# Attention and a mixture of experts on one core: the last three slot tiles behind a branch on the count of tiles in use

## The chip, the core and the metric

The kernel runs on one core of one Trainium2 chip. The metric is the time of one execution in device microseconds (us). Three timed runs of the kernel before gave 283.19, 280.19 and 283.39 us, median 283.19. The profile is of one more execution of 279.71 us.

## What is computed

A chunked attention (32 heads in 4 batches of 8, 768 positions, 64 channels) feeds a mixture of experts over 3072 tokens of 512 channels. Each token goes through a dense two-layer network and through one of 8 experts, chosen by the largest gate logit. The reference, cut to what matters here:

```python
x = attn_out.transpose(0, 2, 1, 3).reshape(B * S, H * D)     # 3072 tokens x 512
y_dense = np.maximum(x @ w1_dense, 0.0) @ w2_dense
logits = x @ w_gate
expert_idx = np.argmax(logits, axis=1)
gate_w = softmax(logits)[np.arange(N), expert_idx]
for e in range(8):
    mask = expert_idx == e
    h = np.maximum(x[mask] @ w1[e], 0.0)
    y_moe[mask] = gate_w[mask, None] * (h @ w2[e])
return y_dense + y_moe
```

The inputs are the same draw each time (a fixed seed), so each expert gets the same tokens in every execution.

## The kernel before

**Order of the work.** All five engines are scheduled by hand: within an engine instructions run in the order in which the kernel's Python emits them. The engines are PE (matrix products), DVE and ACT (element-wise), POOL (element-wise, and DMAs whose descriptors it makes itself), and SP (which here only issues DMAs).

**First 180 us.** The attention of 16 pairs of heads, the dense layers, and the gate. For each token a record (its activations in bf16, its gate weight, its number, its dense result) is written to a table `x_rec` in DRAM, in the row of its expert's region (`row_out`, L480 to L495).

**Slot tiles.** The experts then work on tiles of 128 rows of that table. How the tokens fall on the experts is known only on the chip, so the program holds the largest number of tiles that can be needed: `NS` = 24 + 8 - 1 = 31 slots. The slots come in two rounds. The first round has `R1` = 11 slots (0 to 10), for tiles that the first three batches fill completely; the second has `R2` = 20 (11 to 30), for all that is left. A slot that gets no rows is computed too: it reads some rows, and its destinations lie outside the output, so its scatter writes nothing.

For each slot two lists on the chip give the first row of its tile in `x_rec` and its expert. They come from the counts per expert: `lists_1a` and `lists_1b` for round one, `lists_2a` (L579), `lists_2b` (L586) and `lists_2c` (L608) for round two. `experts_of` (L507) returns `cum`, the running sum of tiles over the experts; its last entry is the count of tiles of that round. The row lists, expert lists and destination offsets are small tiles in SBUF.

An engine that needs an entry as an address reads it into registers: `entry` (L627) loads up to 8 values in one instruction (TENSOR_LOAD; in the profile its line is L632) and hands them out slot by slot. In round one that is 8 and 3 values, in round two 8, 8 and 4; PE, DVE and SP each do it.

One slot s is worked on in these steps:

- `fetch(s)` (L650, SP): a DMA of 128 rows, 385 KB, from `x_rec` into one of the rooms (`room`, L643; round two has 12).
- `transposed(s)` (L672): PE transposes the activations in four pieces into PSUM (`at_ps`, L679), ACT copies them to `xT` (L683).
- `staged(s)` (L686, DVE): copies the expert's first weights to `w_st` (L690); three buffers.
- `first_layer(s)` (L693): 16 matmuls into PSUM (`sc`, L698), then ReLU on ACT (`h_sb`, L703).
- `second_layer(s)` (L706): 4 matmuls with the expert's second weights, at a register's address (`av`, L711), on POOL the destinations (`dst`, L719), on DVE the weighted sum `y` with the dense result (L724), on POOL the scatter of the rows to the output (L727).

In the loop of a round the steps are interleaved: first layer of s, transposes and staging of s + 2, second layer of s - 1, a fetch for a later slot. The first twelve fetches of round two, and staging and transposes of its first two slots, stand ahead of its loop (L907 to L911):

```python
for s in range(R1, NS):
    first_layer(s)
    if s + 2 < NS:
        transposed(s + 2)
        staged(s + 2)
    if s > R1:
        second_layer(s - 1)
        if s - 1 + 2 * T < NS:
            fetch(s - 1 + 2 * T)
second_layer(NS - 1)
```

After the last slot each engine drains and meets the others at a barrier (rows of L948); SP waits there for every DMA's semaphore.

Of the kernel before, what the change touches and what calls it, by code (L numbers as in the profile page):

```python
# [14 lines left out]
ALU = mybir.AluOpType  # L15
AX = mybir.AxisListType
I32 = mybir.dt.int32
# [3 lines left out]
def kernel(  # L21
# [14 lines left out]
    nc = tc.nc  # L36
# [12 lines left out]
    T = S // 128  # L49
# [3 lines left out]
    PE_, DVE_ = mybir.EngineType.PE, mybir.EngineType.DVE  # L53
    ACT_, POOL_, SP_ = (
        mybir.EngineType.Activation, mybir.EngineType.Pool, mybir.EngineType.SP
    )
# [3 lines left out]
    E = moe_w_gate.shape[1]  # L60
# [30 lines left out]
    NS = NT + E - 1  # L91

    R1 = -(-((N_tokens - S) - E * 127) // 128)
    R2 = NS - R1
    r_pool = ctx.enter_context(tc.tile_pool(name="r_pool", bufs=1))

    def iota_f32(n, name, base=0, step=1, cm=0):
# [26 lines left out]
    with (  # L124
# [372 lines left out]
        lst = {}  # L497
# [9 lines left out]
        def experts_of(cnt, n, add):  # L507

            cnt_i = r_work.tile([128, E], I32, tag="cnt_i")
            nc.vector.tensor_scalar(cnt_i, cnt, add, None, ALU.add)  # L510
            nc.vector.tensor_scalar(cnt_i, cnt_i, 7, None, ALU.logical_shift_right)
            tl = r_work.tile([128, 1, E], F32, tag="tl")
            nc.vector.tensor_copy(tl[:, 0], cnt_i)
            part = r_work.tile([128, E, E], F32, tag="part")
            nc.vector.tensor_tensor(part, upto, tl.to_broadcast([128, E, E]), ALU.mult)
            cum = r_work.tile([128, E, 1], F32, tag="cum")
            nc.vector.reduce_sum(cum, part, axis=AX.X)

            en = r_work.tile([128, R2, E], F32, tag="en")
            en = en[:, :n]  # L520
            nc.vector.tensor_tensor(
                en, slot_no[:, :n, None].to_broadcast([128, n, E]),
                cum.rearrange("p e o -> p o e").to_broadcast([128, n, E]), ALU.is_ge,
            )
            ef = r_work.tile([128, R2], F32, tag="ef")
            ef = ef[:, :n]
            nc.vector.reduce_sum(ef, en, axis=AX.X)
            return tl[:, 0], cum, en, ef

        def of_expert(val, en, n, tag):  # L530

            step = r_work.tile([128, 1, E], F32, tag="step")
            nc.vector.tensor_tensor(step[:, 0], val[:, 1:], val[:, :E], ALU.subtract)
            big = r_work.tile([128, R2, E], F32, tag="big")
            big = big[:, :n]
            nc.vector.tensor_tensor(big, en, step.to_broadcast([128, n, E]), ALU.mult)
            got = r_work.tile([128, R2], F32, tag=tag)
            got = got[:, :n]
            nc.vector.reduce_sum(got, big, axis=AX.X)
            return got  # L540
# [38 lines left out]
        def lists_2a():  # L579
# [3 lines left out]
            nc.vector.tensor_tensor(cnt, cnt_ps, low[:, :E], ALU.subtract)  # L583
            lst["b"] = cnt_ps, experts_of(cnt, R2, 127.0)

        def lists_2b():  # L586
            cnt_ps, (tl, cum, en, ef) = lst.pop("b")

            org = r_work.tile([128, E + 1], F32, tag="org")
            nc.vector.memset(org[:, E:], 0.0)  # L590
            nc.vector.scalar_tensor_tensor(
                org[:, :E], cum[:, :, 0], -128.0, cnt_ps, op0=ALU.mult, op1=ALU.add
            )
            rb = of_expert(org, en, R2, "rb")
            nc.vector.scalar_tensor_tensor(
                rb, rb, org[:, 0:1], slot_row[:, :R2], op0=ALU.add, op1=ALU.add
            )

            nc.vector.scalar_tensor_tensor(
                rb, ef, float(E), rb, op0=ALU.is_lt, op1=ALU.mult  # L600
            )
            rb_i = r_pool.tile([128, R2], I32, name="rb_2")
            nc.vector.tensor_copy(rb_i, rb)
            et_i = r_pool.tile([128, R2], I32, name="et_2")
            nc.vector.tensor_scalar(et_i, ef, float(E - 1), None, ALU.min)
            lst["c"] = rb, en, rb_i, et_i

        def lists_2c():  # L608
# [34 lines left out]
        def room(s):  # L643

            if s < R1:
                return bat[B - 2]["rec"], s % T
            j = (s - R1) % (2 * T)
            return bat[B - 1 if j < T else B - 2]["rec"], j % T

        def fetch(s):  # L650
            row = entry(SP_, 0, s, r_sp, N_rows - 128)
            xg, t = room(s)
            ins = nc.sync.dma_start(xg[:, t, :], x_rec[bass.ds(row, 128), :])
            if s in (0, R1):
                while rows_written:
                    tc.add_manual_dep(
                        ins.ins, rows_written.pop(),
                        mybir.DependencyInfo(
                            mybir.DependencyClass.Sync, mybir.DependencyReason.DATA
                        ),  # L660
                        reason="the rows in DRAM",
                    )
            elif s < R1:
                for f in rows_written:
                    tc.declare_no_dep(
                        ins.ins, f, reason="tiles of this round are full without these"
                    )
            xgs[s] = xg, t
            if s < R1:
                first_round.append(ins.ins.name)  # L670

        def transposed(s):  # L672
            xtp = at_b[:, 2 * (s % 2):2 * (s % 2) + 2, :].rearrange(
                "p a (d t) -> p (a d) t", t=128
            )
            xg, t = xgs[s]
            xgb = xg.bitcast(BF16)
            for d in range(DT):
                nc.tensor.transpose(  # L679
                    xtp[:, d, :], xgb[:, t, d * 128:(d + 1) * 128], identity  # L680
                )
            xT = m_work.tile([128, DT, 128], BF16, tag="xT")
            nc.scalar.copy(xT, xtp)  # L683
            xTs[s] = xT

        def staged(s):  # L686

            e = entry(DVE_, 1, s, e_dve, E - 1)
            w_st = w_work.tile([128, DT, F], BF16, tag="w_st")
            nc.vector.tensor_copy(w_st[:, None], w1_all[:, bass.ds(e, 1), :, :])  # L690
            w_sts[s] = w_st

        def first_layer(s):  # L693
            xT, w = xTs.pop(s), w_sts.pop(s)
            ph = sc[:, s % 2, :].rearrange("p (f t) -> p f t", t=128)
            for f in range(FT):
                for d in range(DT):
                    nc.tensor.matmul(  # L698
                        ph[:, f, :], w[:, d, f * 128:(f + 1) * 128], xT[:, d, :],
                        start=(d == 0), stop=(d == DT - 1),  # L700
                    )
            h_sb = m_work.tile([128, FT, 128], BF16, tag="h")
            nc.scalar.activation(h_sb, ph, AF.Relu)  # L703
            hs[s] = h_sb

        def second_layer(s):  # L706
            h_e = hs.pop(s)
            py = av[:, s % 2, :]
            e = entry(PE_, 1, s, e_pe, E - 1)
            for f in range(FT):  # L710
                nc.tensor.matmul(  # L711
                    py, h_e[:, f, :], w2_all[:, bass.ds(e, 1), f, :],
                    start=(f == 0), stop=(f == FT - 1),
                )
            xg, t = xgs.pop(s)
            s0, _, _, _, far_i = lists[s >= R1]

            dst = y_work.tile([128, 1], I32, tag="dst")
            nc.gpsimd.tensor_tensor(  # L719
                dst, xg.bitcast(I32)[:, t, GW + 1:GW + 2], far_i[:, s - s0:s - s0 + 1],  # L720
                ALU.add,
            )
            y = y_work.tile([128, D_moe], F32, tag="y")
            nc.vector.scalar_tensor_tensor(  # L724
                y, py, xg[:, t, GW:GW + 1], xg[:, t, YD:], op0=ALU.mult, op1=ALU.add
            )
            ins = nc.gpsimd.indirect_dma_start(  # L727
                out, bass.IndirectOffsetOnAxis(ap=dst, axis=0), y, None,
                bounds_check=N_tokens - 1, oob_is_err=False,
            )  # L730
            scattered(ins, "out")
# [177 lines left out]
        for s in range(R1, R1 + 2):  # L909
            staged(s)  # L910
            transposed(s)  # L911
        for s in range(R1, NS):
            first_layer(s)
            if s + 2 < NS:
                transposed(s + 2)
                staged(s + 2)
            if s > R1:
                second_layer(s - 1)
                if s - 1 + 2 * T < NS:
                    fetch(s - 1 + 2 * T)  # L920
        second_layer(NS - 1)
        moe.close()


# [28 lines left out]
```

## Time and profile before

| | us |
|---|---|
| median of three timed runs | 283.19 |
| lowest, highest of them | 280.19, 283.39 |
| the profiled execution | 279.71 |
| its span, first to last instruction | 278.0 |
| PE busy | 208.4 (75%) |
| DVE busy | 158.7 (57%) |
| ACT busy | 134.8 (48%) |
| POOL busy | 136.0 (49%) |
| mean granted clock of PE | 0.93 of full speed |

How to read the profile's lines. A group or piece names the engine, the source line, the operation and the tiles it writes and reads; an engine's name with a q is its sequencer, which waits, loads registers and issues, while the engine itself idles. In brackets stands the idle time of the engine before an instruction and what ended it. The chain is the work that ended last, followed back from the last instruction; each piece of it starts when the one before it releases it, and "issue" is time for which the profile shows no releaser.

### The profile page before, as it was taken

How to read it: one execution, taken by the hardware profiler on the slowest of the kernel's cores; microseconds unless marked ns; L12 is line 12 of the kernel's file. 1: busy time of each engine (PE TensorE's matmuls, PEld its weight loads, DVE VectorE, ACT ScalarE, POOL GpSimd, SP SyncE). 2: the span in 40 equal slices, each digit the busy share in tenths (PEclk: the TensorE clock that was granted, in tenths of full speed). 3: DMA queues.
4: the chain of work that ended last, by engine and by line, in shares of the span. 5: the costliest groups of instructions: out<-in, count | busy, mean ns of one | idle time of the engine just before them, and what ended most of it. 6: DMA issues, size and time to landing. Idle time of an engine off the chain costs nothing.

```text
span 278.0 us, 10776 instructions
## 1 busy us (share of the span) xinstructions
PE 208.4 (75%) x4528; PEld 156.1 (56%) x4559; DVE 158.7 (57%) x321; ACT 134.8 (48%) x204; POOL 136.0 (49%) x210
## 2 busy tenths in 40 slices
PE   1487569539878859598686986869879968999970
PEld 1365547337656547375455765637656646777740
DVE  3575476445674566546537575674585555676740
ACT  2273565516556546265535556426653525555520
POOL 8055155512376673075445144640846654756561
PEclk9999795968999988889978699999999999999996
DMA  6999989995999999988999299896988999893310
GB/s 103 187 119 188 194 141 168 199 195 105 183 198 163 223 161 226 194 202 150 191 180 215 39 212 398 205 218 204 346 202 243 309 397 403 265 335 148 120 59 0
DMA packets 59440, 55.51 MB, mean 200 GB/s; under 512 B 35966, under 2 KB 51326, under 8 KB 59392
## 3 DMA queue, kind: packets, MB, share of 16 engines
q0 software_dynamic: 20560, 31.49, 54.7%
q1 hardware_dynamic: 38832, 23.33, 34.9%
q8 instruction: 36, 0.59, 0.9%
q14 instruction: 12, 0.10, 0.1%
HBM read 51.62 MB, written 20.74 MB: 260 GB/s over the span
## 4 chain that ended last, share of the span: by engine, by line
PE 51%; issue 16%; DMA 12%; DVE 9%; ACT 5%; SPq 3%; POOL 1%; POOLq 0%; DVEq 0%; ACTq 0%
DMA vw<-in_v_dram 7%; PE sc L698 7%; PE ph L460 7%; PE av L711 6%; PE pd L474 6%; PE av L311 5%; PE at_ps L299 4%; PE tp_f L241 4%; PE xtt L355 4%; DMA out_dram<-y,dst 3%; PE at_ps L370 2%; PE at_ps L679 2%; PE sc L275 2%; SPq L217 2%; ACT h_d L467 2%
## 5 line engine op out<-in xcount | busy, mean ns | idle before, releaser
L485 POOL DMA_INDIRECT x_rec<-rec_b,row_i x24 | 24.9, 1036 | 50.7 <-issue 28.7
L727 POOL DMA_INDIRECT out_dram<-y,dst x31 | 31.3, 1009 | 27.7 <-DVE w_st L690 12.9
L724 DVE SCALAR_TENSOR_TENSOR y<-av,rec_b 128x512 f32<-128x512 f32 x31 | 23.3, 750 | 23.8 <-PE av L711 17.7
L284 DVE TENSOR_REDUCE mx<-sc 128x12 f32<-128x768 f32 x16 | 15.3, 957 | 35.3 <-PE sc L275 35.3
L698 PEld LDWEIGHTS <-w_st 128*128 128x128 bf16 x496 | 30.2, 98 | 8.3 <-DVE w_st L690 1.1
L698 PE MATMUL sc<-xT,w_st 128*128 128x128 bf16 x496 | 32.8, 219 | 1.6 <-DVE w_st L690 0.9
L311 PE MATMUL av<-vw,at 64*32 64x65 f32 x1536 | 22.6, 240 | 15.1 <-issue 15.0
L711 PE MATMUL av<-w_all,h_sb 128*128 x112 | 30.5, 379 | 4.5 <-DVE y L724 2.4
L703 ACT ACTIVATE h_sb<-sc 128x512 bf16<-128x512 f32 x31 | 18.5, 597 | 31.4 <-PE sc L698 31.4
L311 PEld LDWEIGHTS av<-vw,at 64*32 64x32 f32 x1536 | 18.1, 112 | 23.5 <-issue 22.5
L474 PE MATMUL pd<-w2d,h_d 128*128 128x512 bf16 x77 | 24.7, 396 | 5.3 <-DVE rec_b L478 3.9
L198 ACT COPY vw<-vw 24x1536 f32<-24x1536 f32 x16 | 23.5, 1468 | 9.2 <-DMA vw<-in_v_dram 8.9
L460 PE MATMUL ph<-xTb_b,w1d 128*128 128x128 bf16 x384 | 27.2, 227 | 1.0 <-issue 1.0
L460 PEld LDWEIGHTS <-w1d 128*128 128x128 bf16 x384 | 24.8, 102 | 4.3 <-issue 1.4
L345 POOL CAST rec_b<-x_p 128x768 bf16<-128x768 f32 x16 | 13.4, 838 | 25.6 <-DVE x_p L323 19.2
L363 POOL CAST xTb_b<-xT 128x768 bf16<-128x768 f32 x15 | 12.5, 832 | 22.9 <-ACT xT L358 22.9
L355 PE MATMUL xtt<-identity_f,x_p 128*128 128x128 f32 x96 | 18.0, 314 | 6.8 <-ACT h_d L467 3.1
L253 DVE COPY dT<-tp_f 128x768 bf16<-128x768 bf16 x16 | 15.3, 954 | 13.6 <-PE tp_f L241 13.3
L690 DVE COPY w_st<-w_all 128x2048 bf16 x31 | 21.2, 694 | 2.6 <-issue 2.5
L478 ACT COPY rec_b<-pd 128x512 f32<-128x512 f32 x16 | 9.4, 585 | 25.9 <-PE pd L474 21.1
L251 ACT COPY dT<-tp_f 128x768 bf16<-128x768 bf16 x16 | 12.7, 795 | 18.2 <-PE tp_f L241 18.0
L291 ACT ACTIVATE a_sb<-dif 128x768 f32<-128x768 f32 x16 | 13.5, 845 | 16.1 <-DVE dif L286 16.1
(231 smaller groups left out, 381.6 us busy)
## 6 DMA issues: line engine op xcount, KB each, us to landing
rec_b<-x_rec SPq DMA_DIRECT2D x31, 385.0 KB
w_all<-in_moe_w_dram POOLq DMA_DIRECT2D x16, 512.0 KB, 10.8
vw<-in_v_dram SPq DMA_DIRECT2D x32, 184.0 KB
x_rec<-rec_b SPq DMA_DIRECT2D x1, 3080.0 KB
vw<-in_mem_v_dram SPq DMA_DIRECT2D x32, 48.0 KB
vw<-in_v_dram SPq DMA_DIRECT2D x64, 4.0 KB
w1d<-in_moe_w_dense_dram POOLq DMA_DIRECT2D x1, 512.0 KB
w2d<-in_moe_w_dense_dram POOLq DMA_DIRECT2D x1, 512.0 KB
```

The costliest lines, as they stand in the source:

```text
L198: copy(vt[p0 + CHUNK:p0 + CTX, :NCH, :D], vt[p0:p0 + CTX - CHUNK, 1:NCH + 1, :D],)
L311: nc.tensor.matmul(av[cc * CHUNK:(cc + 1) * CHUNK, hh, t * (D + 1):(t + 1) * (D + 1)], at[p0:p0 + KEYS, t, cc * CHUNK:(cc + 1) * CHUNK], v ...
L355: nc.tensor.transpose(xtt[:, t * 128:(t + 1) * 128], xb[:, t0 + t, :], identity_f32)
L460: nc.tensor.matmul(ph[:, f * 128:(f + 1) * 128], w1d_sb[:, d, f * 128:(f + 1) * 128], xTb[:, d, t * 128:(t + 1) * 128], start=(d == 0), st ...
L474: nc.tensor.matmul(pd, h_d[:, f * 128:(f + 1) * 128], w2d_sb[:, f, :], start=(f == 0), stop=(f == FT - 1),)
L485: ins = nc.gpsimd.indirect_dma_start(x_rec, bass.IndirectOffsetOnAxis(ap=row_i[:, n:n + 1], axis=0), bat[b]["rec"][:, t, :], None,)
L690: nc.vector.tensor_copy(w_st[:, None], w1_all[:, bass.ds(e, 1), :, :])
L698: nc.tensor.matmul(ph[:, f, :], w[:, d, f * 128:(f + 1) * 128], xT[:, d, :], start=(d == 0), stop=(d == DT - 1),)
L703: nc.scalar.activation(h_sb, ph, AF.Relu)
L711: nc.tensor.matmul(py, h_e[:, f, :], w2_all[:, bass.ds(e, 1), f, :], start=(f == 0), stop=(f == FT - 1),)
L724: nc.vector.scalar_tensor_tensor(y, py, xg[:, t, GW:GW + 1], xg[:, t, YD:], op0=ALU.mult, op1=ALU.add)
L727: ins = nc.gpsimd.indirect_dma_start(out, bass.IndirectOffsetOnAxis(ap=dst, axis=0), y, None, bounds_check=N_tokens - 1, oob_is_err=False,)
```

## The change

A constant `NS_MOST` = NS - 3 = 28 is added. In `lists_2b`, DVE computes `used`, the count of tiles in use in both rounds (the last entry of `cum` plus R1), as an integer. Ahead of the second round's loop each of the five engines loads that one value into a register. The loop becomes a function of its first and last slot; it runs once for slots 11 to 27, with fetches up to slot 27. Slots 28, 29 and 30 stand behind a branch that every engine takes for itself, on `used` > 28: three fetches, staging and transposes of the first two, then the same function. In the arm that skips them each engine adds to its semaphores what the body would have added, so that the waits behind it hold in both cases.

In the order of each engine this puts the new load: on PE between the first weight load and the first matmul of slot 11's first layer; on DVE ahead of the staging of slot 13; on ACT ahead of the ReLU of slot 11; on POOL ahead of the destinations of slot 11; on SP behind the fetch of slot 22. The branch stands behind each engine's last instruction for slot 27. The body holds 157 instructions of PE, 15 of DVE, 12 of ACT, 16 of POOL and 13 of SP.

```diff
     R2 = NS - R1
+    NS_MOST = NS - 3
...
             nc.vector.tensor_scalar(et_i, ef, float(E - 1), None, ALU.min)
+
+            used = r_pool.tile([128, 1], I32, name="used")
+            nc.vector.tensor_scalar(used, cum[:, E - 1], float(R1), None, ALU.add)
+            lst["used"] = used
             lst["c"] = rb, en, rb_i, et_i
...
         for s in range(R1, R1 + 2):
             staged(s)
             transposed(s)
-        for s in range(R1, NS):
-            first_layer(s)
-            if s + 2 < NS:
-                transposed(s + 2)
-                staged(s + 2)
-            if s > R1:
-                second_layer(s - 1)
-                if s - 1 + 2 * T < NS:
-                    fetch(s - 1 + 2 * T)
-        second_layer(NS - 1)
+        def slot_tiles(first, end):
+            for s in range(first, end):
+                first_layer(s)
+                if s + 2 < end:
+                    transposed(s + 2)
+                    staged(s + 2)
+                if s > first:
+                    second_layer(s - 1)
+                    if first < NS_MOST and s - 1 + 2 * T < NS_MOST:
+                        fetch(s - 1 + 2 * T)
+            second_layer(end - 1)
+
+        any_more = nc.values_load(
+            lst.pop("used")[0:1, 0:1], engines=(PE_, DVE_, ACT_, POOL_, SP_),
+            min_val=0, max_val=NS,
+            skip_runtime_bounds_check_because="a count of tiles",
+        )
+        slot_tiles(R1, NS_MOST)
+
+        with tc.If(any_more > NS_MOST):
+            for s in range(NS_MOST, NS):
+                fetch(s)
+            for s in range(NS_MOST, NS_MOST + 2):
+                staged(s)
+                transposed(s)
+            slot_tiles(NS_MOST, NS)
         moe.close()
```

## The prediction

> **What bounds the kernel now.** I read the page first (span, chain), then the stretches from 203 us on, the chain in order of time, and the rows of the last instructions. By the page the chain that ends last is half TensorE:
>
> ```profile
> span 278.0 us, 10776 instructions
> PE 51%; issue 16%; DMA 12%; DVE 9%; ACT 5%; SPq 3%; POOL 1%; POOLq 0%; DVEq 0%; ACTq 0%
> ```
>
> The edit touches only what runs after about 203 us, so two stretches matter. The columns are length, then busy time per engine, clock, DMA share, GB/s.
>
> ```profile
> 232.00:264.00 32.00, 31.55 (x379) 24.25 (x386) 21.68 (x32) 17.11 (x33) 19.45 (x30) 1.00 0.69 241
> 264.00:272.00 8.00, 5.33 (x46) 3.13 (x45) 3.03 (x5) 1.90 (x4) 4.97 (x9) 1.00 0.16 55
> ```
>
> From 232 to 264 PE is busy 31.55 of 32.00 us at a granted clock of 1.00: the second round of slot tiles is bound by PE alone, and no other engine is near full. One slot tile is three pieces in the chain:
>
> ```profile
> 258.68 0.89 PE sc L698 x16
> 259.58 0.22 PE at_ps L679 x4
> 259.80 0.86 PE av L711 x4
> 260.66 0.89 PE sc L698 x16
> ```
>
> From one first layer to the next is 260.66 - 258.68 = 1.98 us. What a slot tile less is worth is read here: 1.98 us each.
>
> **Is the branch skipped?** The body runs if more than 28 tiles are in use. In the drawn inputs, by the reference's routing, the experts take 339, 581, 96, 448, 352, 375, 288 and 593 tokens; of the first 2304 tokens 128, 495, 96, 352, 288, 160, 288, 497. Round one takes full tiles in order until it has 11 (1, 3, 0, 2, 2, 1, 2, 0). What is left, rounded up to tiles, is 2, 2, 1, 2, 1, 2, 1, 5 = 16, so 27 are used. The first expert has exactly 128 early tokens; one fewer gives 27 too. The trace agrees. Of the last five output scatters the first two and the last, and what the DMA engines moved from 265 to 278 us in 40 slices of 0.325 us:
>
> ```profile
> 264.21 0.99 POOL L727 DMA_INDIRECT out_dram<-y,dst  x1 [0.78 <-DVE w_st L690]
> 266.19 0.98 POOL L727 DMA_INDIRECT out_dram<-y,dst  x1 [0.77 <-POOL dst L719]
> ...
> 271.79 0.99 POOL L727 DMA_INDIRECT out_dram<-y,dst  x1 [0.66 <-POOL dst L719]
> GB/s 25 0 290 378 139 0 0 0 2 0 0 0 0 0 2 0 0 0 0 0 2 0 0 0 0 1 1 0 0 0 0 0 0 0 0 0 0 0 0 0
> ```
>
> The burst at 265.65 to 266.6 belongs to the scatter of 264.21 (slot 26); the four scatters after it (slots 27 to 30) move nothing. So 27 tiles hold rows, 27 > 28 is false, and slots 28, 29 and 30 go.
>
> **The change, part by part.**
>
> *Three slot tiles removed.* They carry 48 + 12 matmuls in the first and second layer, 12 transposes, six ACT operations, six DVE ones, three scatters on POOL, and three fetches of 385 KB on SP. All but PE's lie beside PE (stretch above), so they cost and give nothing by themselves. The last two slots of the list have no successor to transpose or stage; slots 26 and 27 now take that form, so the tail keeps its shape and moves up by 3 x 1.98 = 5.94 us. Term: -5.94.
>
> *One DVE operation, `used`, 128x1, in the list stage.* It stands behind L605 and ahead of the staging copy:
>
> ```profile
> 203.65 0.17 DVE L605 TENSOR_SCALAR et<-ef 128x20 int32<-128x20 f32 x1
> 203.72 0.69 DVE L690 COPY w_st<-w_all 128x2048 bf16 x1
> 204.62 0.75 DVE L724 SCALAR_TENSOR_TENSOR y<-av,rec_b 128x512 f32<-128x512 f32 x1 [0.21 <-PE av L711]
> ```
>
> At most 0.17 us, and DVE idles 0.21 us before the y that waits for PE, which covers it. Without that cover 0.17 us would enter the chain. Term: 0.
>
> *A register load on each engine.* Where these land decides their price. In the program's order PE's load stands between the weight load of the first matmul of slot 11 (which waits for DVE's staged weights) and that matmul. That is the head of the second round, where the chain reads:
>
> ```profile
> 227.86 0.70 DVE w_st L690
> 228.56 0.05 issue
> 228.61 1.08 PE sc L698 x16
> ...
> 230.42 1.05 PE sc L698 x16
> 231.47 0.22 PE at_ps L679 x4
> 231.70 0.44 issue
> 232.13 0.81 PE av L711 x3
> 232.94 0.89 PE sc L698 x16
> ```
>
> PE waits here for w_st until 228.56, and only then can its sequencer reach the new load. Sixteen matmuls stand behind it, ACT waits for those, and from 232 on PE never idles again, so nothing absorbs the delay: the load is paid in full. The 0.44 us of issue at 231.70 is such a load of eight values, partly covered. The rows of the loads that exist (ns min/median/max; then single ones on PE, of eight values at 230.9 and 246.9 and of four at 262.8):
>
> ```profile
> L632 SPq TENSOR_LOAD <-rb x5: 302/685/1031, 182.5 to 240.7; - x5
> L632 DVEq TENSOR_LOAD <-et x5: 346/601/1740, 193.1 to 256.8; - x5
> L632 PEldq TENSOR_LOAD <-et x5: 332/812/1139, 202.3 to 262.8; - x5
> L632 PEldq TENSOR_LOAD <-et x1: 812/812/812, 230.9 to 230.9; - x1
> L632 PEldq TENSOR_LOAD <-et x1: 587/587/587, 246.9 to 246.9; - x1
> L632 PEldq TENSOR_LOAD <-et x1: 332/332/332, 262.8 to 262.8; - x1
> ```
>
> Eight values less four are 255 ns, 64 ns a value; one value in the quiet end would be 332 - 3 x 64 = 140 ns. That is the lower bound. The upper is the longest load of the trace, 1.74 us. At 230.9, nearest in time and on the same engine, eight values took 0.22 us over the quiet 587 ns; I add 0.25 us for that, and 0.05 us of issue: 0.45 us. Ends kept: 0.14 and 1.74. Term: +0.45.
>
> The Trainium skill, page "Runtime: NRT & Kernel Launch", section "Instruction fetch mechanics", puts a register load at about 200 ns per register even in bulk. The trace disagrees for further values (64 ns); by that figure the term would be an estimated 0.2 us and the gain 0.25 us larger.
>
> The other four loads are hidden, each by its own idle time:
>
> ```profile
> 229.77 0.60 ACT L703 ACTIVATE h_sb<-sc 128x512 bf16<-128x512 f32 x1 [1.40 <-PE sc L698]
> L653 SPq EVENT_SEMAPHORE  x9: 511/1377/4717, 225.9 to 246.2; - x9
> 234.57 0.98 POOL L727 DMA_INDIRECT out_dram<-y,dst  x1 [4.01 <-DMA rec_b<-x_rec]
> ```
>
> ACT idles 1.40 us where its load comes (only one over 1.40 would show). SP's load stands behind the twelfth fetch of the round, where SP next waits 4.72 us for a free room; the five fetches queued behind it lose nothing. POOL's stands ahead of slot 11's scatter, which waits 4.01 us anyway. DVE's stands ahead of the third staging copy; that one is first needed for slot 13 at 232.94, three microseconds later. Term: 0; uncovered, each costs at most the 1.74 above.
>
> *The branch.* Each engine compares and jumps over its body; in the skip arm it adds what the body would have added to its semaphores, and POOL posts one INC_SWDGE_SEM. The trace has no taken branch. The places are all at an engine's end, so the covers are the drains:
>
> ```profile
> L948 POOLq DRAIN  x3: 51/111/5620, 271.6 to 277.7; - x3
> L948 PEldq DRAIN  x2: 13/332/652, 269.6 to 277.5; - x2
> L937 POOLq INC_SWDGE_SEM  x1: 31/31/31, 0.2 to 0.2; - x1
> ```
>
> POOL's drain sets the end: it begins at 271.57, before the last scatter, and ends at 277.19, 4.4 us after that scatter's operation (271.79 + 0.99). PE is there over six microseconds earlier (269.6), ACT and DVE like it; SP jumps even earlier. Only POOL's branch can count. Lower bound 0, if the drain is counted from the scatter; upper bound a fetch of code that nothing covers. For that the nearest rows are a page of code and a DMA's landing in the quiet end:
>
> ```profile
> q8 instruction: 36, 0.59, 0.9%
> DMA to landing us min/median/max: 2.1/2.4/2.7
> ```
>
> 0.9% of 16 x 278 us over 36 packets is 1.1 us a page; 2.7 us is the upper bound. I take 0.1 us, since over 1 us of sequencer time lies beside the scatter. A negative cost I exclude: the skip arm only adds.
>
> **Sum**: -5.94 + 0.45 + 0 + 0.1 = -5.4 us. Against the profiled execution (279.71 us, 1.7 us of it outside the span) that is 274.3 us. The three timed runs are 283.19, 280.19 and 283.39, median 283.19; at that median's level it is 277.8. The profile doesn't say what parts the levels, so I put the forecast between: mean of the four executions 281.6, less 5.4 = **276.2 us**.
>
> **Rivals.**
>
> *POOL's branch is exposed.* If the drain's 5.62 us run from its own start, a code fetch ahead of it is paid: up to +2.7, sum -2.7, 278.9 us. For it: POOL is the last engine, and no row shows how a jump behaves. Against it: POOL's body is 16 instructions long, and the drain outlasts the scatter, which suggests that it waits for the scatter's aftermath. The Trainium skill, same page and section, says that a taken branch to a target outside the current two pages stalls for a DMA fetch; no run here shows one yet. Chance 0.12.
>
> *PE's load is hidden.* If PE's sequencer read it while waiting for w_st, the 0.45 goes: 275.8 us, inside the range. Against it: the load stands behind that wait. Chance 0.1, within the main case.
>
> *The body runs after all: slower.* If the count were over 28, the second round would be cut in two. The first cut shows the price; slot 10's second layer, and the scatter whose buffer its y waits for:
>
> ```profile
> 225.39 1.02 PE L711 MATMUL av<-w_all,h_sb 128*128 x4 [0.84 <-DVE y L724]
> 218.30 8.54 DMA out_dram<-y,dst
> ```
>
> Slot 10's second layer ends at 226.41, slot 11's at 232.94, 6.53 us instead of 1.98. Less the 0.43 us until 226.84, for which y waited for an old scatter, that is +4.1, with the load's 0.45 +4.6 and with a jump of 2.7 at most +7.3: 286.2 to 288.9 us. It decides from 29 used tiles; the trace shows 27. Chance 0.05.
>
> **How the numbers follow.** The main case (skipped, branch covered) has 0.83. Its own range runs from the profiled level with the load at 0.14 (273.9) to the highest run with it at 1.74 (283.39 - 5.94 + 1.74 + 0.1 = 279.3). The exposed branch reaches 280.7 at the highest level; I let half of it out: 273.7 to 279.8. A change of 2% (5.7 us, about what a measurement of this kernel can tell from no change, its runs being 1.1% apart) is nearly the size of the gain: 277.5 divides. The main case falls below it at the lower level and a little above it at the upper, so I give it 0.55 faster and 0.28 same; the exposed branch 0.04 and 0.08; the running body 0.01 same and 0.04 slower. Faster 0.59, same 0.37, slower 0.04.
>
> **What would show it.** In the changed profile: three fewer in each group of L698, L711, L727 (28 scatters); a period still 1.98 us; an issue gap of 0.2 to 1.2 us at slot 11's first matmul, and PE's load beginning after w_st; the last scatter about 5.4 us earlier; POOL's drain ending 4.4 us after it. A drain that ends later by over 1 us makes the first rival right. Thirty-one scatters make the third. If the time moves and the second round's head and tail both stand as said, something outside this account moved.

## The result and the profile after

| | before | changed | ratio, 95% interval |
|---|---|---|---|
| timed runs, us: median (lowest to highest) | 283.27 (280.19 to 286.15) | 275.51 (271.54 to 280.25) | 0.967 [0.959, 0.976] |
| predicted | | 276.2 (273.7 to 279.8) | 0.981 for the sum of -5.4 |

The changed kernel is faster. The ratios and intervals here leave out the slower, disturbed executions, so they are not ratios of the medians (275.51 / 283.27 = 0.973), and since the first profiled execution of the changed kernel (280.25 us) was a disturbed one, as were those of two of the experiments below (`pad` and `pad_again`), the rows after the change are those of a second profile of the same kernel, the run `again`: 275.97 us, span 274.3.

The page's first line, and the chain of waits that ended last:

```profile
span 274.3 us, 10621 instructions
...
POOL 0%; issue 0%
POOL out_dram L732 0%
```

The chain has two short pieces and no more. It is followed back by semaphores and by instructions on one engine, and here it ends at the last scatter, beside the branch. A chain that covers no part of the span doesn't say that POOL bounds the kernel; here the stretches and the timeline have to be read in its place. The second round (same columns as before: length, then PE, PEld, DVE, ACT and POOL, clock, DMA share, GB/s) and two first layers in the middle of it:

```profile
232.00:258.00 26.00, 25.47 (x313) 19.45 (x311) 16.80 (x25) 14.16 (x27) 14.70 (x22) 1.00 0.68 236
```

```profile
250.67 1.06 PE L703 MATMUL sc<-xT,w_st 128*128 128x128 bf16 x16
...
252.65 1.06 PE L703 MATMUL sc<-xT,w_st 128*128 128x128 bf16 x16
```

PE is as full as before, and a slot tile still takes 252.65 - 250.67 = 1.98 us. The scatters' group on the page now counts 28, so three slots are gone:

```profile
L732 POOL DMA_INDIRECT out_dram<-y,dst x28 | 28.1, 1002 | 25.9 <-DVE w_st L695 15.4
```

The new loads (nanoseconds of one, least, median and longest, then the first and last start):

```profile
L929 POOLq TENSOR_LOAD <-used x1: 555/555/555, 229.6 to 229.6; - x1
L929 ACTq TENSOR_LOAD <-used x1: 544/544/544, 229.6 to 229.6; - x1
L929 DVEq TENSOR_LOAD <-used x1: 325/325/325, 229.7 to 229.7; - x1
L929 SPq TENSOR_LOAD <-used x1: 613/613/613, 230.1 to 230.1; - x1
L929 PEldq TENSOR_LOAD <-used x1: 610/610/610, 230.2 to 230.2; - x1
```

The head of the second round in the timeline, where PE's load stands (the idle time of the engine and what ended it in brackets):

```profile
229.50 2.07 DVE L695 COPY w_st<-w_all 128x2048 bf16 x3 [0.51 <-issue]
...
230.25 0.10 PEld L703 LDWEIGHTS <-w_st 128*128 128x128 bf16 x1 [0.94 <-issue]
230.88 1.05 PE L703 MATMUL sc<-xT,w_st 128*128 128x128 bf16 x16 [1.40 <-DVE w_st L695]
230.91 0.85 PEld L703 LDWEIGHTS <-w_st 128*128 128x128 bf16 x15 [0.56 <-issue]
...
232.03 0.60 ACT L708 ACTIVATE h_sb<-sc 128x512 bf16<-128x512 f32 x1 [1.87 <-PE sc L703]
```

The first of the three staging copies ends at 230.20, 0.70 us after its start. One weight load follows at 230.25, then nothing for 0.56 us, then the other fifteen. The first matmul starts at 230.88, 0.68 us after the copy (before: 0.05). Its row still names DVE's copy as what ended the wait, though that was over; the register load is not named as a releaser here, and shows only as the hole in PEld's row.

The end of POOL, from the branch's rows and those of the last barrier:

```profile
267.91 0.98 POOL L732 DMA_INDIRECT out_dram<-y,dst  x1 [0.66 <-POOLq L936]
```

```profile
L936 ACTq COMPARE_BRANCH  x1: 50/50/50, 263.7 to 263.7; - x1
...
L936 PEldq COMPARE_BRANCH  x1: 377/377/377, 265.7 to 265.7; - x1
...
L936 DVEq COMPARE_BRANCH  x1: 72/72/72, 266.4 to 266.4; - x1
...
L936 POOLq COMPARE_BRANCH  x1: 54/54/54, 267.7 to 267.7; - x1
L936 POOLq INC_SWDGE_SEM  x1: 1199/1199/1199, 268.1 to 268.1; - x1
```

```profile
L969 POOLq DRAIN  x3: 46/103/4147, 269.3 to 274.0; - x3
```

POOL's sequencer compares and jumps at 267.7, before the last scatter has started (267.91); INC_SWDGE_SEM runs from 268.1 to 269.3, mostly beside that scatter, which ends at 268.89; the drain takes 4.15 us from 269.3. It ends 4.55 us after the scatter's operation, 0.14 us more than before.

**Where the 5.4 us are.** Measured from the end of slot 11's staging copy (228.56 before, 230.20 after) to the start of the last scatter (271.79 and 267.91) the second round takes 43.23 and 37.71 us: 5.52 less. The end behind it takes 0.14 more. Together 5.4 us, the predicted sum. The timed runs differ by more: the medians by 283.27 - 275.51 = 7.8 us, and the ratio of 0.967 stands for some 9 us. That is the question for the experiments.

### The profile page after: what moved, and what is told of

The parts are those of the page before. It is cut to its first block, busy times and chain, and to the rows that moved or that the text cites. A ratio compares the mean times of both kernels' runs of the same rounds, so it can differ in the third digit from the quotient of the medians.

```text
span 278.5 us, 10591 instructions
## 1 busy us (share of the span) xinstructions
PE 202.6 (73%) x4457; PEld 151.5 (54%) x4487; DVE 155.1 (56%) x316; ACT 131.7 (47%) x198; POOL 133.0 (48%) x204
## 5 line engine op out<-in xcount | busy, mean ns | idle before, releaser
L732 POOL DMA_INDIRECT out_dram<-y,dst x28 | 28.0, 999 | 25.8 <-DVE w_st L695 15.3
L729 DVE SCALAR_TENSOR_TENSOR y<-av,rec_b 128x512 f32<-128x512 f32 x28 | 21.0, 750 | 21.8 <-PE av L716 19.9
L703 PEld LDWEIGHTS <-w_st 128*128 128x128 bf16 x448 | 27.3, 98 | 7.8 <-issue 1.1
L703 PE MATMUL sc<-xT,w_st 128*128 128x128 bf16 x448 | 29.6, 219 | 1.8 <-DVE w_st L695 1.7
L716 PE MATMUL av<-w_all,h_sb 128*128 x101 | 27.5, 379 | 4.1 <-DVE y L729 2.4
L708 ACT ACTIVATE h_sb<-sc 128x512 bf16<-128x512 f32 x28 | 16.7, 597 | 28.4 <-PE sc L703 28.3
L475 PE MATMUL pd<-w2d,h_d 128*128 128x512 bf16 x77 | 25.5, 407 | 5.7 <-DVE rec_b L479 3.7
L461 PEld LDWEIGHTS <-w1d 128*128 128x128 bf16 x384 | 25.4, 104 | 4.6 <-issue 0.9
L300 PE MATMUL at_ps<-identity_f,a_sb 128*128 128x128 f32 x96 | 17.9, 337 | 4.4 <-issue 2.3
```

What stands on the lines that cost most here:

```text
L300: nc.tensor.transpose(at_ps[:, t, :], a_sb[:, t, :], identity_f32)
L461: nc.tensor.matmul(ph[:, f * 128:(f + 1) * 128], w1d_sb[:, d, f * 128:(f + 1) * 128], xTb[:, d, t * 128:(t + 1) * 128], start=(d == 0), st ...
L475: nc.tensor.matmul(pd, h_d[:, f * 128:(f + 1) * 128], w2d_sb[:, f, :], start=(f == 0), stop=(f == FT - 1),)
L703: nc.tensor.matmul(ph[:, f, :], w[:, d, f * 128:(f + 1) * 128], xT[:, d, :], start=(d == 0), stop=(d == DT - 1),)
L716: nc.tensor.matmul(py, h_e[:, f, :], w2_all[:, bass.ds(e, 1), f, :], start=(f == 0), stop=(f == FT - 1),)
L729: nc.vector.scalar_tensor_tensor(y, py, xg[:, t, GW:GW + 1], xg[:, t, YD:], op0=ALU.mult, op1=ALU.add)
```

## The experiments

**Theory A**: all that the edit does lies between slot 11's staging and the end: three periods less, PE's load and the end of POOL more, -5.4 us or 0.981. What the first comparison shows beyond that comes from the stretch ahead of slot 11, which varies from execution to execution. **Theory B**: the new tile `used` moves later tiles in SBUF by 32 bytes (72 of them by the expectations below; the traces show no addresses), and that speeds the stretch ahead of slot 11 by 2 to 4 us. Rivals of single steps: that the load is hidden, that POOL's branch is exposed, that a cut of the round is dear.

In each trace two numbers are read: the stretch from slot 11's staging to the last scatter, and the whole time less the start of that staging (51.85 us before: 279.71 - 227.86).

### The same kernel again, and the edit taken apart

`again` is the changed kernel. `static28` drops the last three slots in the program text, without count, loads or branch; it leaves out slots that hold no rows in this draw:

```diff
-        for s in range(R1, NS):
+        end = NS - 3
+        for s in range(R1, end):
...
-        second_layer(NS - 1)
+        second_layer(end - 1)
```

`noshift` is the changed kernel with `used` inside the tile of the expert list, so that no later tile moves; `pad` is the kernel before with `used` and its one operation alone:

```diff
-            et_i = r_pool.tile([128, R2], I32, name="et_2")
+            et_u = r_pool.tile([128, R2 + 1], I32, name="et_2")
+            et_i, used = et_u[:, :R2], et_u[:, R2:]
...
-            used = r_pool.tile([128, 1], I32, name="used")
```

```diff
+            used = r_pool.tile([128, 1], I32, name="used")
+            nc.vector.tensor_scalar(used, cum[:, E - 1], float(R1), None, ALU.add)
```

> The changed kernel again. Theory A: the edit's own effect is three periods of 1.98 us less PE's load; all of it lies between the end of slot 11's staging copy and the last scatter, 43.24 us in the kernel before and 37.6 +-0.3 here, with POOL's drain ending 4.4 to 4.6 us after the last scatter's operation. What the timed runs show beyond 5.5 us is scatter in the stretch ahead of slot 11, so the time ratio is 0.975 to 0.985 over many runs. Theory B: the stretch ahead of slot 11 is shorter too, because the new 4-byte tile moves nearly every later tile by 32 bytes; then that stretch is 2 to 4 us under that of the kernel before and the ratio is 0.967 again.

> The kernel before with its second round cut to 17 slots in the source: no count, no load, no branch; the three slots without tokens are left out. Theory A: from the end of slot 11's staging copy to the last scatter 43.24 - 5.94 = 37.3 us, 0.3 to 0.5 us less than with the branch, no stall ahead of slot 11's first matmul (0.06 us as before), ratio 0.975 to 0.983. Theory B: the tiles do not move, so the ratio is 0.979, clearly above that of the changed kernel (0.967), although this one does strictly less.

> The changed kernel with the count kept in a spare column of the expert list, so that no tile moves. Theory A: the same as the changed kernel, 37.6 us in the stretch, same ratio within the scatter. Theory B: it loses the 2 to 4 us ahead of slot 11, ratio 0.980.

> The kernel before with only the count computed: the tile (and so the shift by 32 bytes) and its one DVE operation, no load, no branch, 31 slots. Theory A: 43.2 us from slot 11's staging to the last scatter, ratio 0.997 to 1.003 up to scatter. Theory B: ratio 0.985 to 0.993, the gain ahead of slot 11.

| | ratio, 95% interval | staging to last scatter, us | time less start of staging, us |
|---|---|---|---|
| again | 0.977 [0.970, 0.983] | 37.71 | 275.97 - 229.50 = 46.47 |
| noshift | 0.984 [0.977, 0.991] | 37.60 | 279.29 - 232.94 = 46.35 |
| static28 | 0.979 [0.972, 0.985] | 37.14 | 275.73 - 230.21 = 45.52 |
| pad | 0.995 [0.990, 0.999] | 44.07 | 284.29 - 231.61 = 52.68 |

Without the shift the gain is there (0.984), and without count, loads and branch too (0.979). So most of the gain does not need the shift, as B would have it. The interval of `pad` just misses 1, and `again` lies 0.7% under `noshift`: a small effect of the shift was still open, and is tried again below. In `static28` PE goes on where it did before the change:

```profile
230.96 0.90 PEld L698 LDWEIGHTS <-w_st 128*128 128x128 bf16 x16 [0.78 <-DVE w_st L690]
230.96 1.07 PE L698 MATMUL sc<-xT,w_st 128*128 128x128 bf16 x16 [0.61 <-DVE w_st L690]
```

All sixteen weight loads are in one row, with no hole, 0.05 us behind the copy (230.21 + 0.70 = 230.91).

### The load in the middle of the round; one slot more behind the branch

`mid` moves the five loads from the head of the loop into it, to slot 17. `mid_skip4` does that and puts four slots behind the branch:

```diff
             for s in range(first, end):
                 first_layer(s)
...
+                if s == R1 + 6:
+                    more.append(nc.values_load(
+                        lst.pop("used")[0:1, 0:1],
...
-        any_more = nc.values_load(
...
+        any_more = more[0]
```

```diff
-    NS_MOST = NS - 3
+    NS_MOST = NS - 4
```

> The changed kernel with the five loads of the count moved from the head of the second round into slot 17, ahead of a second layer, where PE works without idle time and its sequencer runs ahead. Theory A (PE's load is paid in full at the head): no stall ahead of slot 11's first matmul beyond the 0.06 us of the kernel before, no gap of PE at slot 17, and from slot 11's staging to the last scatter 37.1 to 37.2 us, as with the slots cut in the source (37.14), against 37.6 to 37.7 with the load at the head. Rival (the load costs the same wherever it stands, since it holds up the sequencer): 37.6 again, with a gap of 0.5 us at slot 17.

> As before this one, with four slots behind the branch (count over 27), so that 27 slots are computed and no empty one. Theory A: one more period of 1.98 us, 35.1 to 35.2 us in the stretch, time 7.7 to 8.1 us under the kernel before, ratio 0.970 to 0.976. Rival (the last slot with tokens now ends the kernel, so its scatter's data is waited for): POOL's drain ends 1 to 3 us later than the 4.55 us after the scatter's operation that the changed kernel shows, and the gain shrinks by that.

`mid`: 0.976 [0.965, 0.986], 37.24 us from staging to last scatter, 45.99 us in all from the staging; the first matmul starts 0.06 us behind the staging copy again. The loads of PE and ACT, and the two first layers around PE's:

```profile
L926 PEldq TENSOR_LOAD <-used x1: 310/310/310, 243.5 to 243.5; - x1
...
L926 ACTq TENSOR_LOAD <-used x1: 832/832/832, 244.6 to 244.6; - x1
```

```profile
243.16 1.06 PE L703 MATMUL sc<-xT,w_st 128*128 128x128 bf16 x16
...
245.14 1.06 PE L703 MATMUL sc<-xT,w_st 128*128 128x128 bf16 x16
```

The period with the load in it is 245.14 - 243.16 = 1.98 us: it costs nothing there. At the head the loads cost 37.71 - 37.24 = 0.47 us net. The load is not dear; its place is, behind a wait with nothing queued on PE.

`mid_skip4`: 0.976 [0.967, 0.986], 35.23 us from staging to last scatter, 2.01 less than `mid`: one period. The ratios do not part the two; the stretch does. Its last scatter, unlike before, carries rows, and the drain behind it is not longer (4.50 us after the scatter's operation).

### The body run; work of POOL behind the last scatter

`body_runs` is the changed kernel with a branch that is always taken into the body here (27 > 11), so that the round is cut in two. `pool_late` is the kernel before with two fills of a weight tile that is no longer needed, on POOL behind the last scatter:

```diff
-        with tc.If(any_more > NS_MOST):
+        with tc.If(any_more > R1):
```

```diff
         second_layer(NS - 1)
+        for _ in range(2):
+            nc.gpsimd.memset(w1d_sb, 0.0)
```

> The changed kernel with the branch on a count over 11, so that the body with the last three slots runs. Theory A by the prediction: 4.6 to 7.3 us over the kernel before in the stretch (47.8 to 50.5 us to the last scatter). Rival (only the restart counts, jumps and loads are free): 46 to 47.5 us.

> The kernel before with two memsets on POOL behind the last scatter (they overwrite dense weights that are no longer needed, some 2 to 4 us of POOL's time). Theory A (the drain waits for the aftermath of the last scatter, so POOL has about 4 us there in which added work costs nothing): the drain still ends 4.4 us after the scatter's operation, or right behind the memsets if they take longer. Rival (the drain's 4 to 5 us run from its own start): it ends 4 us after the memsets, so later by their whole length.

`body_runs`: 1.014 [1.002, 1.027] from two runs, 46.38 us from staging to last scatter, 3.14 more than before: what the rival expected, and less than theory A. The cut in its timeline:

```profile
263.88 1.02 PE L716 MATMUL av<-w_all,h_sb 128*128 x4 [0.84 <-DVE y L729]
...
265.61 1.89 DVE L695 COPY w_st<-w_all 128x2048 bf16 x3
...
266.35 1.07 PE L703 MATMUL sc<-xT,w_st 128*128 128x128 bf16 x16 [0.16 <-DVE w_st L695]
...
269.27 0.81 PE L716 MATMUL av<-w_all,h_sb 128*128 x3
```

From slot 27's second layer to slot 28's it is 5.39 us start to start, where the cut ahead of slot 11 took 232.13 - 225.39 = 6.74. The 1.35 less are 0.74 ahead of the staging copy (1.73 against 2.47; ahead of slot 11 y waited 0.43 for an old scatter) and 0.60 behind the first layer's start (2.92 against 3.52; there stood four transposes, 0.22 in the chain, and the wait for a load of eight values).

`pool_late`, one run and one profile: 43.19 us to the last scatter, as before, but the end is another:

```profile
278.81 0.99 POOL L727 DMA_INDIRECT out_dram<-y,dst  x1 [0.66 <-POOL dst L719]
279.78 3.69 POOL L923 MEMSET w1d<- 128x2048 bf16 x2
```

```profile
L950 POOLq DRAIN  x3: 51/111/6243, 281.7 to 288.4; - x3
```

The drain ends at 281.7 + 6.2 = 287.9 us, 8.1 us after the scatter's operation (279.80) but 4.4 us after the last fill (279.78 + 3.69 = 283.47). Before, it ended 4.4 us after the scatter, which was POOL's last operation there. So with a fill last the drain ends some 4.4 us after the fill, and the scatter's aftermath doesn't set it. From the start of the staging this execution takes 290.43 - 234.92 = 55.51 us, 3.66 more than before: the fills' 3.69 us are paid, as the rival expected.

### The shift once more, and the two best versions on one chip

`pad_again` is `pad`; `shift64` makes its tile 64 bytes wide; `changed_again` and `mid_skip4_again` repeat two kernels beside each other:

```diff
-            used = r_pool.tile([128, 1], I32, name="used")
-            nc.vector.tensor_scalar(used, cum[:, E - 1], float(R1), None, ALU.add)
+            used = r_pool.tile([128, 16], I32, name="used")
+            nc.vector.tensor_scalar(used[:, 0:1], cum[:, E - 1], float(R1), None, ALU.add)
```

> The kernel before with the tile used and its one operation, and neither loads nor branch; a second, longer comparison, since the first gave a ratio of 0.9947 with an interval of 0.990 to 0.999. Theory A (all of the gain lies between slot 11's staging and the end): ratio 1.000, in an interval that holds 1. The rival that a shift of 72 later tiles by 32 bytes is worth a part: ratio 0.995 again, some 1.5 us, gained ahead of slot 11. From slot 11's staging to the last scatter both expect before's 43.2 us.

> As pad_again, with the tile 64 bytes wide in place of 4 (its operation writes one column of it, as there), so that the later tiles are shifted by 64 bytes and not by 32. Theory A: the same as pad_again and as before, 1.000. The rival that the place matters: another ratio than pad_again's; if it is a question of a boundary of 64 bytes, 1.000 here beside 0.995 there.

> The changed kernel once more, beside its shorter form on one chip. Theory A: 5.5 us less than before, 0.980 to 0.981; the 0.967 of the first comparison would need some 9 us, of which 3.6 are nowhere in the stretch that the change touches. The rival of the shift: 0.975, 7 us.

> The load in the middle of slot 17's work and four slots behind the branch, beside the changed kernel on one chip. Theory A: 0.56 us less for the load that PE no longer waits for and 2.0 us less for a period, so 2.5 us under changed_again: 0.971 to 0.973 against before. The rival that the last tile's own work was bound elsewhere (its scatter now carries rows): no more than 0.6 us under changed_again.

| | ratio, 95% interval | staging to last scatter, us | time less start of staging, us |
|---|---|---|---|
| pad_again | 1.004 [0.996, 1.013] | 43.20 | 289.77 - 237.97 = 51.80 |
| shift64 | 0.995 [0.987, 1.003] | 43.09 | 278.65 - 226.97 = 51.68 |
| changed_again | 0.987 [0.980, 0.995] | 38.59 | 278.46 - 231.12 = 47.34 |
| mid_skip4_again | 0.964 [0.955, 0.974] | 35.55 | 271.11 - 226.85 = 44.26 |

`pad` is 0.995 in one comparison and 1.004 in the other: no effect of the shift is left that these runs can tell from none. The extra 0.9 us of `changed_again`'s second round goes with its granted clock, 0.96 there against 1.00 in `again`:

```profile
231.80:270.40 38.60, 35.20 (x400) 26.46 (x400) 22.57 (x34) 17.30 (x32) 22.69 (x34) 0.96 0.58 208
```

```profile
230.20:267.90 37.70, 34.08 (x400) 25.28 (x400) 22.74 (x33) 17.29 (x32) 22.39 (x34) 1.00 0.60 214
```

The same 400 matmuls take 35.20 - 34.08 = 1.12 us more. `mid_skip4` is the fastest kernel of this study, 274.13 us median beside 278.53 of the changed kernel on the same chip; from slot 11's staging on it is 47.34 - 44.26 = 3.1 us less, 2.5 of them expected. Without the 0.9 us that go with the clock of `changed_again`, 2.2 are left: `mid_skip4_again` itself takes 0.32 us longer in the stretch than `mid_skip4`. In one of its periods, 2.11 us long (y at 245.82 and 247.93), the second layer starts 0.35 us behind the transposes (246.52 and 246.87) where 0.22 is usual, and a later load of eight values ends between the two (246.08 to 246.66): in a full queue, too, a long load can cost a little. That its last scatter carries rows, and `again`'s none, shows in the 2 us from 1 us behind its start on (columns: length, busy POOL, clock, DMA share, GB/s):

```profile
264.10:266.10 2.00, 0.00 (x0) 0.85 0.35 133
```

```profile
268.91:270.91 2.00, 0.00 (x0) 0.50 0.02 0
```

It is shown for this draw alone: with 28 tiles in use its body would run, and the branch that runs its body cost 3.1 us in `body_runs`.

## Why the prediction was right, step by step

The time (275.51 for 276.2) and the sign came out as forecast, and in the traces so did the sum, with one step that rested in part on a wrong reason. That the time is met to 0.7 us is luck: the level was put at 281.6, 1.7 us under the median of 283.27 that the comparison gave, and the timed difference is 2.4 us larger than the sum.

**What bounds: right.** The second round is PE's alone, and a slot less is worth a period. `static28` and `mid_skip4` show it without the loads' cost mixed in (6.09 us for three, with 0.17 from the load of eight values, told below; 2.01 for one).

**Three slots, -5.94: right.** Slot 11's y and the last y on DVE, before and in `again`:

```profile
233.04 0.75 DVE L724 SCALAR_TENSOR_TENSOR y<-av,rec_b 128x512 f32<-128x512 f32 x1 [2.51 <-DMA rec_b<-x_rec]
...
270.26 0.75 DVE L724 SCALAR_TENSOR_TENSOR y<-av,rec_b 128x512 f32<-128x512 f32 x1 [1.11 <-PE av L711]
```

```profile
235.08 0.75 DVE L729 SCALAR_TENSOR_TENSOR y<-av,rec_b 128x512 f32<-128x512 f32 x1 [2.42 <-PE av L716]
...
266.37 0.75 DVE L729 SCALAR_TENSOR_TENSOR y<-av,rec_b 128x512 f32<-128x512 f32 x1 [1.11 <-PE av L716]
```

Between them, where the load is already behind, the round shrank from 37.22 us to 31.29, by 5.93.

**PE's load, +0.45: right in place, a little small.** The wait of the first matmul behind the staging copy grew from 0.05 us to 0.68 in `again`, and to 0.56 and 0.54 in the first profile and in `noshift`: +0.5 to +0.6. The load took 610 ns in `again`, 491 in the first profile, 387 in `body_runs` and 310 in `mid`, so the length of 0.14 us that was worked out for one value, and kept as the lower bound, is not seen anywhere: the step of 64 ns a value from eight to four does not go on to one. The term came out near because the 0.25 us added for a busy place made up for that; over the 310 ns of `mid` the busy places add 0.08 to 0.30. The rival that the load is hidden is refuted by the hole in PEld's row and by `mid`.

**What the prediction did not have: -0.2.** From slot 11's staging to its y the round takes 4.88 us (235.08 - 230.20) instead of 4.48 (233.04 - 228.56), 0.4 more and not 0.6. Between them, ahead of slot 11's second layer, lies PE's load of eight values. It took 812 ns before and 599 in `again`, 0.21 less. The later start does not cover it: in both it begins 0.48 us behind the start of slot 12's first layer (230.90 - 230.42, 233.16 - 232.68). Leaving out `pad` and `changed_again`, which had a lower clock there, the time from staging to y is in ten of twelve profiles the first matmul's wait, plus this load, plus 3.60 to 3.63 us. With PE's new load at the head the load of eight took 597 to 648 ns in five profiles, without it 633 to 812 in nine; why, no run shows. `static28` has 645 ns and so 0.17 us of this too. So -5.93 + 0.62 - 0.2 gives the 5.5 us of the stretch. The 0.44 us that the prediction read as this load's wait include a matmul whose record is missing: the row counts three of four, and by the weight loads the first one starts some 0.2 us earlier.

**The other four loads and `used`, 0: right.** ACT's load of 544 ns starts at 229.6, beside ACT's copy of the transposes and ahead of an idle time of 1.87 us, and `mid`'s loads of up to 832 ns (on ACT) left the period at 1.98. `static28` has none of this and is faster by 46.47 - 45.52 = 0.95 us: 0.57 in the stretch, which PE's load covers, and 0.39 at the end.

**The branch, +0.1: right in size; of its two reasons one failed.** It measured 0.14: the drain ends 4.41 us after the scatter's operation in the profiles of before, `pad`, `pad_again` and `shift64`, and 4.55 in the five with a jump over three slots. Against `static28`, whose drain ends 4.16 us after its scatter, it is 0.39; why that end is shorter is open. The reason given with the term, that over 1 us of sequencer time lies beside the scatter, held in the main: the jump was over before the last scatter began, that scatter came after the same idle time as before (0.66 us), and INC_SWDGE_SEM lay beside it for all but 0.4 us of its 1.2.

The step that failed is the reason given against the first rival: "the drain outlasts the scatter, which suggests that it waits for the scatter's aftermath". In `pool_late` the drain ends 4.4 us after POOL's last operation, a fill, and the fills are paid. The first rival is not right as it stands either: a drain of 4.15 (`again`), 5.62 (before) and 6.24 us (`pool_late`) has no fixed length from its own start. It was right that work behind the last scatter can lengthen the end. Its price did not show: the jump took 50 to 72 ns on ACT, DVE and POOL. PE's took 377 ns (90 in `body_runs`, where it is not taken) at 265.7, with only the last second layer left to PE and over 2 us ahead of the last scatter. The Trainium skill, page "Runtime: NRT & Kernel Launch", section "Instruction fetch mechanics", has a taken branch out of the two loaded pages stall for a fetch. No stall that anything waited for shows here; whether a jump over 157 instructions of PE, or 16 of POOL, leaves those pages, the traces don't show.

**The running body, 286.2 to 288.9: too dear.** Measured with the body run: +3.1 us in the round, a ratio of 1.014, and no jump to pay. The price was taken from the first cut, whose wait for an old scatter was deducted, but neither the rest of the wait ahead of its staging nor the transposes and the load of eight values behind its first layer. The last three slots ahead of a cut give back some more, since their periods are 1.87 us and not 1.98 (before: 271.79 - 266.19 = 5.60 for three). It is still on the slower side, by 1.4%, with an interval that reaches beyond 2%.

**The level: open.** The timed difference was 7.8 us, or some 9 by the ratio, for a sum of 5.4. From the start of slot 11's staging on, the first profile (280.25 - 233.87 = 46.38 us), `again` and `noshift` agree to 0.1 us, and before, `shift64` and `pad_again` to 0.2 (51.68 to 51.85); `changed_again` and `pad`, which don't fit, had a mean granted clock of 0.96 in the second round. The stretch ahead of it, in which these kernels do the same work but for one 0.15 us operation, started slot 11's staging at 226.85 (`mid_skip4_again`), 226.97 (`shift64`), 227.86 (before), 231.12 (`changed_again`) and 232.94 us (`noshift`), with no order by kernel. The granted clock of that stretch does not order them either (0.89 in `shift64`, 0.90 in `noshift` and `changed_again`, 0.93 before). Three comparisons of the changed kernel gave 0.967, 0.977 and 0.987, on average 0.977 or 6.5 us, and the intervals of the first and the third don't meet. So the prediction's 5.4 us stand on the traces, and a ratio from one such comparison can be off by about 1%, as these three show, a little more than its interval says. What varies ahead of slot 11 is not settled; that it is the place of the tiles was tried and not found.

## What to carry to other kernels

A register load costs its engine what stands idle behind it: put it where its queue is full, not behind the wait that heads a new phase. When POOL ends the program, look at what its sequencer still does behind its last operation, and count the final drain from that operation. To judge a change of 2% in a kernel whose early part scatters by as much, measure from a fixed event ahead of the change to the end in each trace, and compare those stretches.

## What the runs showed of the hardware

- POOL's closing drain ended 4.16 to 4.55 us after POOL's last operation: a scatter without rows (4.41 before, 4.16 in `static28`, 4.55 in `again` with a branch between), one with rows (4.50 in `mid_skip4`, with a branch between) or a fill (4.42 in `pool_late`).
- A load of one value into a register took 310 to 832 ns in `mid` and 325 to 613 in `again`, hardly less than one of four values on PE (332 ns before): most of the price comes with the first value.
- INC_SWDGE_SEM took 31 ns at the program's start and 1199 behind a scatter.
- The timeline shows instructions of a sequencer beside or ahead of the engine's operation that stands before them in the program: POOL's jump at 267.7, the scatter ahead of it at 267.91.
